# Routed experts with 1,632 slots, odd-sized ones as a double-width matmul, in a fused attention and mixture-of-experts kernel

## The chip, the cores and the metric

One core of one Trainium2 chip runs the whole program. The metric is the device time of one execution in microseconds (us). The kernel before takes 794.46 us, the median of 3 runs (794.2 to 794.81). A core has one matrix engine (TensorE, PE in the profile; its weight loads are listed apart as PEld), VectorE (DVE), ScalarE (ACT), GpSimd (POOL) and SyncE (SP), which here only issues transfers. Each engine works off its own list of instructions in order and waits on semaphores for the others.

## The reference

Three layers follow each other, all in fp32. The third is the one that the change touches: each of 1,536 tokens goes to the one of 8 experts whose logit is largest, and only that expert's two weight matrices (512 by 1024 and 1024 by 512) act on it.

```python
x = attention(q, k, v, lam)                 # (1536, 512), decayed, in blocks of 64
out1 = sum_e p[:, e] * (relu(x @ w1[e]) @ w2[e])          # 4 experts, every token
logits = out1 @ w_gate                      # (1536, 8)
expert = argmax(logits); gate = softmax(logits)[expert]
for e in range(8):
    xe = out1[expert == e]
    out[expert == e] = gate[expert == e] * (relu(xe @ w1b[e]) @ w2b[e])
```

With the reference's inputs the eight experts get 161, 102, 158, 127, 272, 269, 247 and 200 tokens.

## The kernel before

Every fp32 operand is split into a high part and a low part in a reduced format (names that end in h and l), and a product is three matmuls into one PSUM bank: high by high, low by high, high by low (`mm3`, L335). Attention and the first mixture fill the time up to about 604 us. Then the routed experts run one after the other, in what is called turns here, 0 to 7.

The tokens' rows are scattered into `bins` in memory, where each expert has a fixed number of slots. Turn 0 is always expert 0; the other seven are ranked by their number of tokens at run time, `BY_RANK` (L36) gives the slots by rank and `TURNS` (L37) the order. So the slots by turn, `CAPS`, are 256, 288, 128, 288, 256, 256, 256, 128: 1,856 in all. A token beyond its expert's slots goes to a loop at the end (L1042 onwards) that runs only where there are such tokens.

A turn has a first product (tiles `g`, or `gr` where the slots are 128) and a second. In the first, weights stand in the array and the slots' columns move past them: 8 banks of PSUM, each 12 matmuls as wide as the slots (`moe2_mm1`, L883). ACT takes relu out of each bank as the high part, DVE subtracts to get the low part (`relu_split`, L343). The second product has two forms. Where the slots fill whole tiles of 128 (`CAPS[e] <= 2 * P`, L1029), the slots stand and the weights move, 512 columns at a time (`moe2_mm2_rows`, tiles `zr`; 48 matmuls for 256 slots), and DVE applies the gate (L947). For 288 slots the weights stand again (`moe2_mm2`, tiles `z`, 4 banks), ACT copies each bank out, PE transposes it back (`yo`, L976) and DVE applies the gate (L978). The PSUM banks of both products come from one ring of three (`ps_mm`).

What else sets the order: between matmul groups the hooks (`hook1`, `hook2`, L999 and L1006) issue the weights' splits, each a copy on ACT (L161) and a subtraction on DVE (L163) of 512 columns, 16 for each expert. `hook1` runs after each of the 8 banks and asks for 2 splits of this turn's second weights; `hook2` runs four times in the second product and asks for the next turn's weights, after two calls also for half of the next turn's second weights where the form is `zr`. Raw weights wait in 6 buffers of 512 KB; a split that frees one makes SP issue the next load. `rows_T` (L870) transposes the next turn's rows on PE (`xt`), and ACT and DVE split them (`xgh`, `xgl`).

Of the kernel before, what the change touches and what calls it, by code (L numbers as in the profile page):

```python
# [18 lines left out]
P = 128  # L19
# [6 lines left out]
DM = H * D  # L26
KD = DM // P
E1, FF = 4, 1024
E2 = 8
HF = FF // 2  # L30
FC = HF // P
# [1 line left out]

BY_RANK = [288, 288, 256, 256, 256, 128, 128]  # L36
TURNS = [0, 5, 1, 2, 3, 4, 6]  # L37
CAPS = [256] + [BY_RANK[i] for i in TURNS]
NSS = [-(-c // P) for c in CAPS]
STS = [c // n for c, n in zip(CAPS, NSS)]  # L40
CAP, ST, NS = CAPS[0], STS[0], NSS[0]
MOST, NMOST = max(CAPS), max(NSS)
W = DM + 2
FAR = 1 << 20
OMAX = (N - min(CAPS[0], BY_RANK[0]) + P - 1) // P
# [4 lines left out]
def body(ctx: ExitStack, tc: tile.TileContext, lam, att, dp, w1a, w2a, wg, wgt, w1b, w2b, out):  # L50
    nc = tc.nc
    V, A, G, T, SP = nc.vector, nc.scalar, nc.gpsimd, nc.tensor, nc.sync
# [282 lines left out]
    def mm3(ps, parts, first, last):  # L335


        ops = [(l, rh) for (lh, ll), (rh, rl) in parts for l in (lh, ll)]
        ops += [(lh, rl) for (lh, ll), (rh, rl) in parts]
        for i, (l, r) in enumerate(ops):  # L340
            T.matmul(ps, l, r, start=first and i == 0, stop=last and i == len(ops) - 1)  # L341

    def relu_split(ps, tag, n, nm, pl, bufs, most=None):  # L343
        hh, hl = (
            pl.tile([P, most or n], F32R, tag=tag + x, name=nm + x, bufs=bufs)[:, :n]
            for x in "hl"
        )
# [289 lines left out]
    with tc.manual_schedule():  # L637
# [15 lines left out]
            out=upper, in_=upper, compare_op=ALU.is_ge, fill=1.0, base=0,  # L653
# [157 lines left out]
        y, z = NC - 2, NC - 1  # L811
# [19 lines left out]
        gx = z_ctx.enter_context(pool("gx", 2))  # L831

        def rows_tiles(e):
            return tuple(
                gx.tile([P, KD, MOST], F32R, tag="xg" + x, name=f"xg{x}{e}")[:, :, :CAPS[e]]
                for x in "hl"
            )

        def rows_split(hi, lo, ps):
            A.copy(out=hi, in_=ps)  # L840
# [2 lines left out]
        xg = {0: rows_tiles(0)}  # L843
# [4 lines left out]
        gp = z_ctx.enter_context(pool("gp", 2))  # L848
# [21 lines left out]
        def rows_T(e, s):  # L870
            if e >= E2:
                return
            if s == 0:
                xg[e] = rows_tiles(e)
            hi, lo = xg[e]
            st = STS[e]
            tr = ps_tr.tile([P, KD, P], F32, tag="tr", name=f"xt{e}_{s}")[:, :, :st]
            for d in range(KD):
                T.transpose(tr[:, d, :], xb_t[e][:st, s, d * P:d * P + P], ident[:st, :st])
            c = slice(s * st, s * st + st)  # L880
            rows_split(hi[:, :, c], lo[:, :, c], tr)

        def moe2_mm1(e, f):  # L883
            hi, lo = xg[e]
            k, c = 2 * (E1 + e) + f // FC, (f % FC) * P
            wh, wl = wt[0, k]
            n = CAPS[e]
            ps = ps_mm.tile([P, 512], F32, tag="mm", name=f"g{e}_{f}")
            mm3(
                ps[:, :n],  # L890
                [((wh[:, d, c:c + P], wl[:, d, c:c + P]), (hi[:, d, :], lo[:, d, :]))
                 for d in range(KD)],
                True, True,
            )
            return relu_split(ps[:, :n], "g", n, f"g{e}_{f}", gp, 2 * FC + 2, MOST)


        def moe2_mm1_rows(e, h, hook):
            hi, lo = xg[e]
            wh, wl = wt[0, 2 * (E1 + e) + h]  # L900
            n = CAPS[e]
            ps = ps_mm.tile([P, 512], F32, tag="mm", name=f"gr{e}_{h}")
            for d in range(KD):
                mm3(ps[:n], [((hi[:, d, :], lo[:, d, :]), (wh[:, d, :], wl[:, d, :]))],
                    d == 0, d == KD - 1)
                if d < KD - 1:
                    hook(h * KD + d)
            g = gp.tile([P, HF], F32, tag="gr", name=f"gr{e}_{h}")
            A.activation(out=g[:n], in_=ps[:n], func=AF.Relu)
            hook(h * KD + KD - 1)  # L910
            return g
# [13 lines left out]
        def moe2_mm2_rows(e, hs, y, hook):  # L925
            st, ns, xb = STS[e], NSS[e], xb_t[e]
            step = FC * ns // 2
            ps = [
                ps_mm.tile([P, 512], F32, tag="mm", name=f"zr{e}_{s}") for s in range(ns)
            ]  # L930
            i = 0
            for h in range(2):
                wh, wl = wt[1, 2 * (E1 + e) + h]
                for s in range(ns):
                    for f in range(FC):
                        hh, hl = hs[h * FC + f]
# [9 lines left out]
                    m = DM // 2 if e == E2 - 1 and s == ns - 1 else DM  # L946
                    V.tensor_scalar(  # L947
                        out=y[:st, s, :m], in0=ps[s][:st, :m], scalar1=gate, scalar2=None,
                        op0=ALU.mult,
                    )  # L950
                    if m < DM:
                        A.activation(
                            out=y[:st, s, m:], in_=ps[s][:st, m:], func=AF.Copy, scale=gate
                        )
                    scatter(out, xb.bitcast(I32)[:st, s, DM + 1:W], y[:st, s, :], N, "out")
            hook(3)


        def moe2_mm2(e, hs, m):
            n = CAPS[e]  # L960
            ps = ps_mm.tile([P, 512], F32, tag="mm", name=f"z{e}_{m}")
            c = slice(m * P, m * P + P)
            parts = []
            for f, (hh, hl) in enumerate(hs):
                wh, wl = wt[1, 2 * (E1 + e) + f // FC]
                parts.append(((wh[:, f % FC, c], wl[:, f % FC, c]), (hh, hl)))
            mm3(ps[:, :n], parts, True, True)
            yt = gp.tile([P, MOST], F32, tag="yt", name=f"yt{e}_{m}", bufs=3)
            A.copy(out=yt[:, :n], in_=ps[:, :n])
            return yt  # L970

        def moe2_out(e, yt, m, y):
# [9 lines left out]
            if m == KD - 1:  # L982
                for s in range(ns):
                    scatter(out, xb.bitcast(I32)[:st, s, DM + 1:W], y[:st, s, :], N, "out")

        load_rows(0)
        load_rows(1)
        raws[:] = [raw2] * 2 + [rawp] * 4
# [3 lines left out]
        for e in range(E2):  # L992
            k = 2 * (E1 + e)
            load_rows(e + 2)
            y = gp.tile([P, NMOST, DM], F32, tag="y", name=f"y{e}")
            hs = []
            turns = []

            def hook1(i):  # L999
                if late:  # L1000
                    late.pop()()
                split_to(1, k + 1, 2)
                if i == KD + 1 and turns:
                    hs.extend(turns.pop()())

            def hook2(i):  # L1006
                if turns:
                    hs.extend(turns.pop()())
                if late:
                    late.pop()()  # L1010
                if e == 0 and i == 0:
                    route_rest()
                if e + 1 < E2:
                    if i < NSS[e + 1]:
                        rows_T(e + 1, i)
                    if CAPS[e] <= 2 * P and i > 1:
                        split_to(1, k + 2, 3)
                    else:
                        split_to(0, k + 3, 2 if i == 0 else 3)

            if CAPS[e] <= P:
                for h in range(2):
                    g = moe2_mm1_rows(e, h, hook1)
                    turns.append(lambda h=h, g=g: moe2_turn(e, h, g))
            else:
                for f in range(2 * FC):
                    hs.append(moe2_mm1(e, f))
                    hook1(f)
            if CAPS[e] <= 2 * P:  # L1029
# [171 lines left out]
```

## Time and profile before

| | before |
|---|---|
| median of 3 runs | 794.46 us |
| profiled execution | 795.49 us |
| its span, first to last instruction | 793.7 us |
| PE busy in the span | 777.6 us (98%) |
| DVE busy in the span | 364.9 us (46%) |
| ACT busy in the span | 218.0 us (27%) |
| mean granted TensorE clock | 0.996 |

The span lies inside the profiled execution, 1.8 us shorter. PE's busy share is taken from records with modelled ends that overlap each other; the distance from the start of one matmul to the start of the next is what a matmul costs in a stream.

### The profile page before, as it was taken

To read this page: it belongs to the slowest core of one execution; us is meant where nothing else is said; L and a number is where in the kernel's file an instruction comes from. 1 tells how busy PE (TensorE), PEld (TensorE's weight loads), DVE (VectorE), ACT (ScalarE), POOL (GpSimd) and SP (SyncE) were. 2 spreads that over 40 slices of the span, in tenths; PEclk is the share of its full clock that TensorE was granted. 3 is DMA by queue.
4 is the path that set the end of the run, shared out by engine and by line. 5 is a ranking of instruction groups with operands and counts; after the bars stand their busy time and mean duration, and the time that the engine had idled before them with its cause. 6 is when DMAs were issued, how large, how long until landed. Compare 5 with 4: busy or idle time off the path is not lost. (4 is left out here: it accounts for less than half of the span.)

```text
span 793.7 us, 11237 instructions
## 1 busy us (share of the span) xinstructions
PE 777.6 (98%) x4458; PEld 649.4 (82%) x4458; DVE 364.9 (46%) x803; ACT 218.0 (27%) x440; POOL 112.1 (14%) x115
## 2 busy tenths in 40 slices
PE   7999999999999999999999999999999999999995
PEld 6788777887777777877777787878888898998884
DVE  5443212232332232233233233689877757677653
ACT  3222222111111221121022131011134546555552
POOL 4463201000110110010011020011120003121101
PEclk9999999999999999999999999999999999999998
DMA  8763273110100010011001012000023867766550
GB/s 271 262 211 122 69 255 130 40 54 1 53 28 27 27 53 27 0 54 54 0 27 54 26 40 67 0 27 27 29 82 132 290 207 264 247 214 225 182 189 24
DMA packets 25431, 81.20 MB, mean 102 GB/s; under 512 B 3164, under 2 KB 5212, under 8 KB 25248
## 3 DMA queue, kind: packets, MB, share of 16 engines
q1 hardware_dynamic: 23232, 74.15, 28.1%
q0 software_dynamic: 2144, 6.31, 2.0%
q8 instruction: 36, 0.59, 0.3%
q14 instruction: 19, 0.16, 0.1%
HBM read 69.40 MB, written 11.70 MB: 102 GB/s over the span
## 5 line engine op out<-in xcount | busy, mean ns | idle before, releaser
L341 PE MATMUL h<-xh,w0h 128*128 128x512 f32 (+1 forms) x432 | 158.3, 373 | 0.7 <-ACT xh L303 0.7
L341 PE MATMUL h<-xh,w0l 128*128 128x512 f32 (+1 forms) x432 | 157.1, 370 | 0.7 <-POOL w0l L163 0.7
L382 DVE SCALAR_TENSOR_TENSOR acc<-y,p_sb,acc 128x512 f32<-128x512 f32 x84 | 63.1, 751 | 124.4 <-PE y L341 122.3
L341 PE MATMUL h<-xl,w0h 128*128 128x512 f32 (+1 forms) x432 | 107.4, 370 | 0.0
L341 PEld LDWEIGHTS h<-xh,w0h 128*128 128x128 f32 x432 | 81.1, 188 | 17.0 <-ACT xh L303 0.9
L341 PEld LDWEIGHTS h<-xh,w0l 128*128 128x128 f32 x432 | 81.2, 188 | 16.4 <-POOL w0l L163 1.1
L341 PEld LDWEIGHTS h<-xl,w0h 128*128 128x128 f32 x432 | 76.2, 188 | 15.2
L348 ACT ACTIVATE ht_0h<-h 128x512 fp32r<-128x512 f32 (+1 forms) x27 | 14.9, 551 | 241.0 <-PE h L341 241.0
L163 POOL TENSOR_TENSOR w0l<-raw,w0h 128x512 fp32r<-128x512 f32 x17 | 22.7, 1340 | 252.1 <-ACT w0h L161 252.1
L161 ACT CAST w1h<-raw 128x512 fp32r<-128x512 f32 x96 | 54.3, 618 | 1.3 <-PE zr L341 1.3
L161 ACT CAST w0h<-raw 128x512 fp32r<-128x512 f32 x96 | 54.0, 620 | 0.5 <-DMA raw<-in_w1a 0.5
L163 DVE TENSOR_TENSOR w1l<-raw,w1h 128x512 fp32r<-128x512 f32 x80 | 52.5, 695 | 2.9 <-ACT w1h L161 2.9
L163 DVE TENSOR_TENSOR w0l<-raw,w0h 128x512 fp32r<-128x512 f32 x79 | 50.9, 687 | 5.8 <-ACT w0h L161 5.4
L341 PE MATMUL g<-xgh,w0h 128*128 128x256 f32 (+1 forms) x192 | 49.7, 289 | 0.6 <-DVE g_0l L349 0.3
L341 PE MATMUL g<-xgh,w0l 128*128 128x256 f32 (+1 forms) x192 | 49.3, 286 | 0.0
L96 POOL DMA_INDIRECT out<-y,xb x16 | 23.2, 1449 | 153.0 <-DVE y L947 64.8
L349 DVE SCALAR_TENSOR_TENSOR ht_0l<-h,ht_0h 128x512 fp32r<-128x512 f32 (+1 forms) x27 | 17.1, 632 | 59.1 <-ACT ht_0h L348 59.1
L341 PE MATMUL y<-w1h,ht_0h 128*128 128x512 f32 x96 | 39.4, 410 | 0.0
L341 PE MATMUL y<-w1h,ht_3l 128*128 128x512 f32 x96 | 39.2, 408 | 0.1
L434 DVE CUSTOM_DVE_ANT_0 jl<-acc,wgb 128x512 f32<-128x512 f32 x56 | 38.4, 685 | 0.8
L341 PE MATMUL y<-w1h,ht_2h 128*128 128x512 f32 x96 | 38.2, 398 | 0.0
L341 PE MATMUL y<-w1h,ht_2l 128*128 128x512 f32 x96 | 38.1, 397 | 0.0
(284 smaller groups left out, 1408.9 us busy)
## 6 DMA issues: line engine op xcount, KB each, us to landing
raw<-in_w1b SPq DMA_DIRECT2D x32, 512.0 KB, 5.4
raw<-in_w2b SPq DMA_DIRECT2D x32, 512.0 KB, 4.7
att<-in_att SPq DMA_DIRECT2D x24, 512.0 KB, 4.9
raw<-in_w2a SPq DMA_DIRECT2D x16, 512.0 KB, 3.6
raw<-in_w1a SPq DMA_DIRECT2D x14, 512.0 KB, 3.5
bins<-fill SPq DMA_DIRECT2D x1, 4626.0 KB, 21.8
xb<-bins SPq DMA_DIRECT2D x4, 514.0 KB, 5.4
wgb<-in_wgt SPq DMA_DIRECT2D x1, 2048.0 KB, 9.7
```

The lines of the kernel that those rows point to most:

```text
L96: i = G.indirect_dma_start(out=dst, out_offset=bass.IndirectOffsetOnAxis(ap=idx, axis=0), in_=src, in_offset=None, bounds_check=rows - 1, ...
L161: A.copy(out=hi, in_=t)
L163: (G if i < 3 else V if i >= 4 * ROUTED else los[i % 2]).tensor_tensor(out=lo, in0=t, in1=hi.bitcast(F32), op=ALU.subtract)
L341: T.matmul(ps, l, r, start=first and i == 0, stop=last and i == len(ops) - 1)
L348: A.activation(out=hh, in_=ps, func=AF.Relu)
L349: V.scalar_tensor_tensor(out=hl, in0=ps, scalar=0.0, in1=hh.bitcast(F32), op0=ALU.max, op1=ALU.subtract)
L382: V.scalar_tensor_tensor(out=acc[:, t, 0:DM], in0=ps, scalar=p_sb[:, t, e:e + 1], in1=acc[:, t, 0:DM], op0=ALU.mult, op1=ALU.add,)
L434: V.tensor_tensor_reduce(out=jl, in0=acc[:, t, 0:DM], in1=rt["wgb"][:, e, :], scale=1.0, scalar=0.0, op0=ALU.mult, op1=ALU.add, accum_out= ...
```

## The change

The slots become 176 for turn 0 and 288, 128, 288, 256, 208, 160, 128 for the others: 1,632. `WIDE` is true for more than 128 and less than 256 slots, turns 0, 5 and 6. For these the high and low activations lie side by side in one tile (`both`), so that `product` multiplies the high weights by both at once (one matmul of twice the slots) and the low weights by the high part (one matmul of the slots, into the first half of the bank): 2 matmuls for 3. The two halves of the bank must then be added: ACT copies the second half out, DVE adds the first (`s`), and relu and the low part read `s` from SBUF. They are put behind the copy and sum of the next bank, through the list `relu`. The wide turns' second product takes the transposed form (`z`). The other turns keep `mm3`. `zr` results are now scaled by the gate on ACT, not DVE. In wide turns `hook1` issues 1 split for each bank instead of 2, `hook2` 2 each time, and only turns with whole tiles (`BY_ROWS`) split the next turn's second weights ahead.

```diff
-BY_RANK = [288, 288, 256, 256, 256, 128, 128]
+BY_RANK = [288, 288, 256, 208, 160, 128, 128]
-CAPS = [256] + [BY_RANK[i] for i in TURNS]
+CAPS = [176] + [BY_RANK[i] for i in TURNS]
+BY_ROWS = [c % P == 0 for c in CAPS]
+WIDE = [P < c < 2 * P for c in CAPS]
...
+        def product(e, ps, parts):
+            n = CAPS[e]
+            if not WIDE[e]:
+                mm3(ps[:, :n], [(w, x[:2]) for w, x in parts], True, True)
+                return ps[:, :n]
+            for i, ((wh, wl), (hi, _, both)) in enumerate(parts):
+                T.matmul(ps[:, :2 * n], wh, both, start=i == 0, stop=False)
+                T.matmul(ps[:, :n], wl, hi, start=False, stop=i == len(parts) - 1)
+            s = gp.tile([P, MOST], F32, tag="yt", name=f"s{ps.name}", bufs=4)[:, :n]
+            A.copy(out=s, in_=ps[:, n:2 * n])
+            V.tensor_tensor(out=s, in0=ps[:, :n], in1=s, op=ALU.add)
+            return s
...
+            relu.append(finish)
+            while len(relu) > WIDE[e]:
+                relu.pop(0)()
...
-                    V.tensor_scalar(
-                        out=y[:st, s, :m], in0=ps[s][:st, :m], scalar1=gate, scalar2=None,
-                        op0=ALU.mult,
-                    )
+                    A.activation(out=y[:st, s, m:], in_=ps[s][:st, m:], func=AF.Copy, scale=gate)
...
-                split_to(1, k + 1, 2)
+                split_to(1, k + 1, 1 if WIDE[e] else 2)
...
-                    if CAPS[e] <= 2 * P and i > 1:
+                    if BY_ROWS[e] and i > 1:
                         split_to(1, k + 2, 3)
                     else:
-                        split_to(0, k + 3, 2 if i == 0 else 3)
+                        split_to(0, k + 3, 2 if i == 0 or WIDE[e] else 3)
```

In the listings that follow a row is the line, the instruction, output<-inputs and the output's size. The first place is PE at the start of turn 0's second product; before:

```order
L341 MATMUL zr_0_5123<-w1h_4976,g_0h 128x512
L341 MATMUL zr_0_5123<-w1h_4976,g_0l 128x512
L341 MATMUL zr_0_5123<-w1l_4977,g_0h 128x512
L341 MATMUL zr_0_5123<-w1h_4976,g_1h 128x512
L341 MATMUL zr_0_5123<-w1h_4976,g_1l 128x512
L341 MATMUL zr_0_5123<-w1l_4977,g_1h 128x512
```

The same place of the changed kernel, where `g_0` is the tile that holds both parts:

```order
L892 MATMUL z_0_5106<-g_0_4970,w1h_4971 128x352
L893 MATMUL z_0_5106<-g_0_4970,w1l_4972 128x176
L892 MATMUL z_0_5106<-g_1_4987,w1h_4971 128x352
L893 MATMUL z_0_5106<-g_1_4987,w1l_4972 128x176
L892 MATMUL z_0_5106<-g_2_5006,w1h_4971 128x352
L893 MATMUL z_0_5106<-g_2_5006,w1l_4972 128x176
```

Three matmuls of 512 columns have become two of 352 and 176, and one output bank now takes all 8 activation tiles in a row instead of 4.

The second place is DVE in turn 0's first product, from the last step of the routing's order (`nth`) on; before, `w1l` are splits of the second weights and `g_0l` the low part of bank 0:

```order
L601 TENSOR_SCALAR nth<-who 128x7
L349 SCALAR_TENSOR_TENSOR g_0l<-g_0_4959,g_0h 128x256
L163 TENSOR_TENSOR w1l_4977<-raw_4600,w1h_4976 128x512 x2
L349 SCALAR_TENSOR_TENSOR g_1l<-g_1_4984,g_1h 128x256
L163 TENSOR_TENSOR w1l_4977<-raw_4637,w1h_4976 128x512 x2
L349 SCALAR_TENSOR_TENSOR g_2l<-g_2_5007,g_2h 128x256
```

In the changed kernel `sg_0` is the sum of bank 0's halves:

```order
L605 TENSOR_SCALAR nth<-who 128x7
L896 TENSOR_TENSOR sg_0_4958_4967<-g_0_4958,sg_0_4958_4967 128x176
L167 TENSOR_TENSOR w1l_4972<-raw_4600,w1h_4971 128x512
L896 TENSOR_TENSOR sg_1_4975_4984<-g_1_4975,sg_1_4975_4984 128x176
L914 SCALAR_TENSOR_TENSOR g_0_4970<-sg_0_4958_4967,g_0_4970 128x176
L167 TENSOR_TENSOR w1l_4972<-raw_4600,w1h_4971 128x512
L896 TENSOR_TENSOR sg_2_4994_5003<-g_2_4994,sg_2_4994_5003 128x176
L914 SCALAR_TENSOR_TENSOR g_1_4987<-sg_1_4975_4984,g_1_4987 128x176
L167 TENSOR_TENSOR w1l_4972<-raw_4637,w1h_4971 128x512
```

Each bank now has two DVE instructions for one, a bank's low part stands behind the next bank's sum, and one split stands between banks for two, so the eighth split comes after the last bank instead of the fourth.

The third place is ACT between turns 4 and 5 in the changed kernel, where `w0h` and `w1h` are splits and `y<-zr` is the gate, which stood on DVE before:

```order
L165 CAST w0h_6349<-raw_6182 128x512 x2
L980 ACTIVATE y_6123<-zr_0_6294,xb_5604 128x512
L980 ACTIVATE y_6123<-zr_1_6295,xb_5604 128x512
L165 CAST w1h_6395<-raw_6206 128x512 x2
L165 CAST w1h_6395<-raw_6228 128x512
L895 COPY sg_0_6418_6427<-g_0_6418 128x208
```

The three splits and the copy of turn 5's bank 0 now queue behind the gate of the last `zr` bank.

## Rows read from the trace of the kernel before

**Rows 1.** The page: span, busy times, TensorE and its granted clock in 40 slices.

```profile
span 793.7 us, 11237 instructions
...
PE   7999999999999999999999999999999999999995
...
PEclk9999999999999999999999999999999999999998
```

**Rows 2.** Windows, turns 0, 2, 3, 5, 6, 7: length, engines' busy, clock, DMA share, GB/s.

```profile
610.47:634.09 23.62, 23.62 (x156) 21.37 (x157) 17.97 (x46) 13.64 (x31) 0.97 (x1) 1.00 0.75 259
...
660.96:675.26 14.30, 13.79 (x74) 11.07 (x72) 10.97 (x19) 11.21 (x23) 7.19 (x3) 1.00 0.91 300
675.26:703.20 27.94, 27.63 (x210) 27.31 (x209) 18.51 (x34) 14.65 (x31) 2.38 (x1) 1.00 0.61 215
...
726.93:750.22 23.29, 23.29 (x153) 21.10 (x152) 15.42 (x29) 12.55 (x26) 2.20 (x2) 1.00 0.61 214
750.22:773.08 22.86, 22.86 (x150) 20.71 (x148) 14.96 (x28) 12.51 (x27) 3.17 (x3) 1.00 0.58 201
773.08:793.70 20.62, 12.53 (x57) 9.46 (x55) 7.34 (x12) 5.00 (x9) 2.14 (x2) 0.86 0.07 28
```

**Rows 3.** Timeline of PE, turns 1 and 6: start, length, instruction, where stages begin.

```profile
634.09 0.29 PE L341 MATMUL g<-xgh,w0h 128*128 128x288 f32 x1
...
646.88 0.30 PE L341 MATMUL z<-g_0h,w1h 128*128 128x288 f32 x1
...
750.22 0.28 PE L341 MATMUL g<-xgh,w0h 128*128 128x256 f32 x1
...
761.53 0.40 PE L341 MATMUL zr<-w1h,g_0h 128*128 128x512 f32 x1
...
764.31 0.60 PE L879 MATMUL xt<-ident,xb 128*128 128x128 f32 x4
764.66 0.48 PE L341 MATMUL zr<-w1h,g_0h 128*128 128x512 f32 x1
```

**Rows 4.** Timeline of PE, narrow matmuls: the routing's logits, and transposes in turn 1.

```profile
577.79 0.95 PE L455 MATMUL lg<-wg_sb,xt 128*128 128x8 f32 x8
578.60 0.63 PE L442 MATMUL rtr<-ident,acc 128*128 128x128 f32 x4
...
653.68 0.49 PE L976 MATMUL yo<-ident,yt 128*96 128x128 f32 x3
653.93 0.38 PE L341 MATMUL z<-g_0h,w1h 128*128 128x288 f32 x1
```

**Rows 5.** Timeline of DVE, start of turn 0.

```profile
611.32 0.15 DVE L582 COPY count<-counts 128x8 f32<-128x8 f32 x1
...
613.01 0.42 DVE L349 SCALAR_TENSOR_TENSOR g_0l<-g,g_0h 128x256 fp32r<-128x256 f32 x1
613.35 1.28 DVE L163 TENSOR_TENSOR w1l<-raw,w1h 128x512 fp32r<-128x512 f32 x2
614.55 0.42 DVE L349 SCALAR_TENSOR_TENSOR g_1l<-g,g_1h 128x256 fp32r<-128x256 f32 x1
```

**Rows 6.** Timeline of ACT, turn 0, turn 2 and the last gate.

```profile
612.24 0.39 ACT L348 ACTIVATE g_0h<-g 128x256 fp32r<-128x256 f32 x1 [1.46 <-issue]
612.52 1.13 ACT L161 CAST w1h<-raw 128x512 fp32r<-128x512 f32 x2
...
661.26 3.22 ACT L161 CAST w1h<-raw 128x512 fp32r<-128x512 f32 x6
...
786.18 0.48 ACT L952 ACTIVATE y<-zr,xb 128x256 f32<-128x256 f32 x1 [4.18 <-DVE y L947]
```

**Rows 7.** Who waited for whom on PE and PEld, 610 to 790 us: total, times, longest.

```profile
PE g L341 <- DVE g_0l L349: 0.3, 1, 0.3
...
PEld zr L341 <- DVE gtl L841: 1.6, 3, 0.9
```

**Rows 8.** SP's own queue, who it waited for, 600 to 794 us.

```profile
SPq L135 <- DVE w0l L163: 88.5, 27, 11.0
```

More of the change, by code (lines that the diff above doesn't have):

```diff
@@ L341, in mm3, with relu_split @@
             T.matmul(ps, l, r, start=first and i == 0, stop=last and i == len(ops) - 1)
-    def relu_split(ps, tag, n, nm, pl, bufs, most=None):
+    def relu_split(ps, tag, n, nm, pl, bufs):
         hh, hl = (
-            pl.tile([P, most or n], F32R, tag=tag + x, name=nm + x, bufs=bufs)[:, :n]
+            pl.tile([P, n], F32R, tag=tag + x, name=nm + x, bufs=bufs)
             for x in "hl"
@@ L833, in rows_tiles @@
         def rows_tiles(e):
-            return tuple(
-                gx.tile([P, KD, MOST], F32R, tag="xg" + x, name=f"xg{x}{e}")[:, :, :CAPS[e]]
-                for x in "hl"
-            )
+            n = CAPS[e]
+            both = gx.tile([P, KD, 2 * MOST], F32R, tag="xg", name=f"xg{e}")[:, :, :2 * n]
+            return both[:, :, :n], both[:, :, n:], both
         def rows_split(hi, lo, ps):
@@ L874, in rows_T @@
                 xg[e] = rows_tiles(e)
-            hi, lo = xg[e]
+            hi, lo, _ = xg[e]
             st = STS[e]
@@ L881, in rows_T @@
             rows_split(hi[:, :, c], lo[:, :, c], tr)
+        def product(e, ps, parts):
+            n = CAPS[e]
+            if not WIDE[e]:
[8 more added lines that the diff above has]
+            return s
         def moe2_mm1(e, f):
-            hi, lo = xg[e]
+            hi, lo, both = xg[e]
             k, c = 2 * (E1 + e) + f // FC, (f % FC) * P
@@ L888, in moe2_mm1, with finish @@
             ps = ps_mm.tile([P, 512], F32, tag="mm", name=f"g{e}_{f}")
[L889 to L895, printed above, removed]
+            s = product(e, ps, [
+                ((wh[:, d, c:c + P], wl[:, d, c:c + P]),
+                 (hi[:, d, :], lo[:, d, :], both[:, d, :])) for d in range(KD)
+            ])
+            g = gp.tile([P, 2 * MOST], F32R, tag="g", name=f"g{e}_{f}", bufs=2 * FC + 2)
+            hh, hl = g[:, :n], g[:, n:2 * n]
+            def finish():
+                A.activation(out=hh, in_=s, func=AF.Relu)
+                V.scalar_tensor_tensor(
+                    out=hl, in0=s, scalar=0.0, in1=hh.bitcast(F32), op0=ALU.max,
+                    op1=ALU.subtract,
+                )
+            relu.append(finish)
+            while len(relu) > WIDE[e]:
+                relu.pop(0)()
+            return hh, hl, g[:, :2 * n]
         def moe2_mm1_rows(e, h, hook):
-            hi, lo = xg[e]
+            hi, lo, _ = xg[e]
             wh, wl = wt[0, 2 * (E1 + e) + h]
@@ L935, in moe2_mm2_rows @@
                     for f in range(FC):
-                        hh, hl = hs[h * FC + f]
+                        hh, hl = hs[h * FC + f][:2]
                         c = slice(s * st, s * st + st)
@@ L945, in moe2_mm2_rows @@
                     gate = xb[:st, s, DM:DM + 1]
-                    m = DM // 2 if e == E2 - 1 and s == ns - 1 else DM
-                    V.tensor_scalar(
-                        out=y[:st, s, :m], in0=ps[s][:st, :m], scalar1=gate, scalar2=None,
-                        op0=ALU.mult,
[L950 to L953, printed above, removed]
+                    m = DM // 2 if e == E2 - 1 and s == ns - 1 else 0
+                    if m:
+                        V.tensor_scalar(
+                            out=y[:st, s, :m], in0=ps[s][:st, :m], scalar1=gate, scalar2=None,
+                            op0=ALU.mult,
                         )
+                    A.activation(out=y[:st, s, m:], in_=ps[s][:st, m:], func=AF.Copy, scale=gate)
                     scatter(out, xb.bitcast(I32)[:st, s, DM + 1:W], y[:st, s, :], N, "out")
@@ L963, in moe2_mm2 @@
             parts = []
-            for f, (hh, hl) in enumerate(hs):
+            for f, h in enumerate(hs):
                 wh, wl = wt[1, 2 * (E1 + e) + f // FC]
[L966 to L969, printed above, removed]
+                parts.append(((wh[:, f % FC, c], wl[:, f % FC, c]), h))
+            s = product(e, ps, parts)
+            if WIDE[e]:
+                return s
+            yt = gp.tile([P, MOST], F32, tag="yt", name=f"yt{e}_{m}", bufs=4)
+            A.copy(out=yt[:, :n], in_=s)
             return yt
@@ L984, in moe2_out @@
                     scatter(out, xb.bitcast(I32)[:st, s, DM + 1:W], y[:st, s, :], N, "out")
+        relu = []
         load_rows(0)
@@ L1027, in body @@
                     hs.append(moe2_mm1(e, f))
+                    if f == 2 * FC - 1:
+                        while relu:
+                            relu.pop(0)()
                     hook1(f)
-            if CAPS[e] <= 2 * P:
+            if BY_ROWS[e]:
                 moe2_mm2_rows(e, hs, y, hook2)
```

## The prediction

> **What bounds the kernel now.** I read the page first: PE is busy in every slice from the second to the last but one, at the upper clock level throughout [rows 1]. So the change is worth what it takes off PE, less what other engines then fail to hide. Next the windows, one for each turn of the routed stage [rows 2]: in the turns that change (0, 5, 6) PE is busy for the whole 23.62, 23.29 and 22.86 us, DVE for 18.0, 15.4 and 15.0, ACT for at most 13.6. PE is the bound, but DVE in turn 0 is only 5.6 us behind, and the change takes work from PE and gives some to DVE. What waits there are on PE and its weight loads from 610 us on are short and name DVE, the largest 1.6 us in all [rows 7]. PE, DVE and ACT wait for no transfer there: it is SP that waits for DVE to free a raw buffer, 88.5 us behind first-weight splits alone [rows 8], and turn 2 took in 300 GB/s [rows 2] without a wait for data.
>
> **What a matmul costs.** From start to start. 256 columns: turn 6's first product is 96 matmuls in 761.53 - 750.22 = 11.31 us, 0.118 each. 288 columns: turn 1's, 96 in 646.88 - 634.09 = 12.79, 0.133 each. 512 columns: 12 in 764.31 - 761.53 = 2.78, 0.232 each [rows 3]. On the line between the last two, 320, 352 and 416 columns are 0.147, 0.161 and 0.190. The narrow partners (160, 176, 208) are not in the trace. Below: by columns alone, 0.46 ns each as at 256, they are 0.074, 0.081, 0.096. Above: the 0.118 of 256 columns. In between stands the row for the logits: 8 matmuls of only 8 columns take 578.60 - 577.79 = 0.81 us, 0.101 each [rows 4], so there is a floor that is not the columns'; each brings a new 128-column weight load, as each narrow partner does. I take 0.101 for all three.
>
> The Trainium skill, TensorE: Matmul & The Clock Gate, section LDWEIGHTS, gives a load the number of its columns over 1.2 ns, whatever the rows; for 128 columns an estimate from that page is 0.107 us. It speaks against a part of this change, since narrower slots then save nothing on the second matmul; the logits' row agrees within 6%. By it the sum below would lose 192 times 0.006, 1.2 us more.
>
> **Part by part: PE.** A wide turn has 32 pairs in each product, 64 in all. Turn 0: 64 x (0.161 + 0.101) = 16.8 us. Turn 5: 64 x 0.291 = 18.6. Turn 6: 64 x 0.248 = 15.9. Before, each was 96 x 0.118 + 48 x 0.232 = 22.4. New are 8 transposes back for each turn; three cost 653.93 - 653.68 = 0.25 us [rows 4], so 0.67. Saved: 22.4 - 16.8 - 0.7 = 4.9, then 3.1 and 5.8, together 13.9 us.
>
> Smaller items. Selecting and placing turn 0's rows is narrower (176 for 256): the last selection, one pair of placing matmuls, one cast and one subtraction stand in a chain before turn 0 and each loses some 0.05 to 0.08 us; 0.3. Row transposes for turns 5 and 6 have 104 and 80 columns for 128, which cost 0.35 for four [rows 3]: 0.1 and 0.25, 0.35 together. The gate leaves DVE in turn 2, so turn 3's bank 0 is split earlier, and the one wait of PE on `g_0l`, 0.3 us [rows 7], goes (in turn 3 PE is 0.3 short of fully busy [rows 2]). Gain in all: 13.9 + 0.3 + 0.35 + 0.3, about 14.9 us.
>
> **Part by part: what DVE and ACT then fail to hide.** In a stream a 512-column split is 0.60 on DVE (two in 614.55 - 613.35) and a 256-column one 0.34 (613.35 - 613.01) [rows 5], so 176 columns are 0.26, 160 0.24, 208 0.29. On ACT it is 0.52 for 512 (six in 3.22) and 0.28 for 256 (612.52 - 612.24) [rows 6], so 0.20 for 176. One bank of turn 0's first product is then 4 x 0.262 = 1.05 on PE, 0.60 + 2 x 0.26 = 1.12 on DVE, 0.92 on ACT. In turn 5: 1.16, 1.18, 0.98. In turn 6: 0.99, 1.08, 0.88. DVE is the slower one, by little, and the ring of three banks lets PE run three banks ahead. What counts is the end of the stage: the second product's first bank reads all 8 tiles and, for its last pair, the eighth split, which now stands last on DVE.
>
> Turn 0: DVE comes late, since the routing's order keeps it until 613.01 [rows 5], 612.4 after the narrower casts; 8 x 0.60 + 16 x 0.26 = 9.0 us more make 621.4. PE starts at 610.2 and could finish this bank at 610.2 + 8.4 + 2.1 = 620.7. It ends about 621.9: 1.2 us lost. Turn 6: DVE starts some 1.5 us in (a bank, ACT's copy), has 9.0 us with one gate of turn 5, so 10.5; PE could be through at 10.1 and ends near 10.9: 0.8 lost. Turn 5: turn 4 still splits three ahead, so five splits are left, and DVE is done with them by bank 4; the end of the chain (copy, sum, relu, low part: some 1.6 us) lies behind six pairs of PE, 1.7 us. The gate on ACT waits for turn 4's last bank, and behind it queue three splits and bank 0's copy; the sum comes some 3.3 us into the turn, when PE needs that bank again at 3.5. Lost: 0. Turn 7: turn 6 no longer splits ahead, so its first ACT relu and DVE's `gtl` queue behind all 8 second-weight splits. Turn 2 is in that place already and takes 14.3 us; without its three row transposes (0.35 x 96/128 each, 0.8) and one more transpose back (0.25) that is 13.2, against the 12.5 for which PE is busy in turn 7 [rows 2]. With DVE later than there I take 1.2 lost.
>
> In the second products DVE has per bank a sum (0.26), a gate (0.34), two splits (1.2) and in some a row split (0.47 for 384 columns, on the same line), 1.8 to 2.3 us, against PE's 2.0 to 2.7 with transposes: hidden. In turn 0 eight small steps of the routing's rest come on top, as long as the eight of its order, 1.7 us [rows 5]; DVE is then about a bank behind, which the ring takes; if it didn't, turn 0 would cost up to 1 us more. Turn 1 loses its splits from turn 0 but has 1.6 us of PE for 1.57 of DVE in each of four banks: hidden. Loads: 8 pieces of 512 KB in some 17 us are 240 GB/s, under turn 2's 300: hidden. Losses: 1.2 + 0.8 + 1.2 = 3.2 us; the bounds are none, if the waits overlap better, and twice that.
>
> **The sum.** 14.9 - 3.2 = 11.7 us. The span goes from 793.7 to 782.0 and the profiled execution from 795.5 to 783.8. The runs' median lies 1.0 below the profiled one, so 782.7.
>
> **Rivals.**
>
> 1. The narrow partners cost their columns alone. 64 x (0.027 + 0.020 + 0.005) = 3.3 us less PE; half of it lies in first products where DVE decides, so 1.7, and with half of the losses gone 779.4. For it: nothing shows that this operand format loads as slowly as that of the logits; the PEld records overlap too much to say. Against: the floor in rows 4.
> 2. DVE becomes the bound of the wide turns. If sums, subtractions and splits don't stream but cost their full length (0.42 at 256 columns and 1.28 - 0.60 = 0.68 at 512 in rows 5, so 0.34 for 176), a bank of turn 0 is 1.36 on DVE for my 1.12, 0.24 more, and so in the others: over 8 banks 1.9 us in turn 0, 1.9 in turn 6 and over 5 banks 1.2 in turn 5, together 5.0: 787.7. For it: each sum now waits for ACT's copy and each relu for the sum. Against: rows 5 show them streaming, and the delay by one bank keeps the two from meeting.
> 3. The clock falls: slower than before. The stalls come at the second product's start in turns 0 and 6 and in turn 7. If they are long enough for the granted clock to go to 1.2 GHz for half of the 51 us of matmuls in the wide turns (16.8 + 18.6 + 15.9), that half takes twice as long, 25 us more: 808. It decides against the change when about 12 us run at the lower level. For it: the last window, where PE stops for 8 us, has clock 0.86. Against: 1.00 in turns 2 and 3, with 0.5 and 0.3 us of PE idle [rows 2], and my stalls are about 1 us. The Trainium skill, TensorE: Matmul & The Clock Gate, section HAM oscillation, has kernels whose engine fell back to half rate between bursts of matmuls.
> 4. The slots don't suffice, and the change doesn't do what it says: one expert with a token too many runs the loop at the end, with its fill, 12 scatters and 4 MB of weights, none of it hidden. At turn 2's 300 GB/s the weights alone are 14 us, and 12 scatters at 0.97 (turn 0's one in rows 2) are 12: at least 808. Against: the counts fit (161 in 176, 200 in 208, 158 in 160; 127 in 128 as before).
>
> **Chances.** Forecast 0.63, rival 1 0.12, rival 2 0.20, rival 3 0.03, rival 4 0.02. What can be told from no change is 0.2%, 1.6 us. The first three are all faster, less 0.02 for a sum of losses that I don't see, hence faster 0.93, same 0.02, slower 0.05. The forecast's own bounds: the narrow partner at 0.118 costs 64 x 3 x 0.017 = 3.2 us more, no losses 3.2 us less. The range reaches to rival 1 with some over and just past rival 2: 778.5 to 788.
>
> **What would show it.** Matmul starts in the wide turns: the narrow partner takes 0.10 us (right), under 0.09 (rival 1) or 0.12 (my upper bound). Turns 0, 5 and 6 take about 19.5, 19.8 and 17.7 us; turn 7 is 1.2 longer. PE waits for DVE at the first `z` bank of turns 0 and 6, on the last `w1l` or `g`, and hardly in turn 5 or inside later banks; waits at each bank would be rival 2. The clock stays at 1.00 in turns 0 to 6. I would be wrong if PE waited for a raw load anywhere from turn 1 on, or if the wide matmul were off the line of the other widths.

## The result, and the profile after

| | before | after |
|---|---|---|
| median of 4 runs each | 794.53 us (794.2 to 794.81) | 785.67 us (785.13 to 787.97) |
| ratio, 95% interval | 1 | 0.9895 (0.9883 to 0.9907) |
| profiled execution / its span | 795.49 / 793.7 us | 785.84 / 783.9 us |
| PE busy | 777.6 us | 766.7 us |
| DVE / ACT busy | 364.9 / 218.0 us | 368.8 / 226.8 us |

The change makes the kernel 8.9 us faster, by 1.05%. I had forecast 782.7 us: sign and mechanism hold, the gain is smaller. All ratios here leave out executions that ran far longer than the rest of the same kernel: six of the twelve of `slots_only` (815 to 817 us, mean granted clock 0.966 to 0.968) and two of the four of `partner64` (798 and 799 us, 0.978 and 0.975), of which no trace is on record, so that where their clock fell stays open, one of `kept` (4055.82 us) and two of the kernel before (1657.25 and 2689.3 us).

The page of the profile after, against [rows 1]: span, busy times, PE and its granted clock in 40 slices.

```profile
span 783.9 us, 11270 instructions
...
PE 766.7 (98%) x4434; PEld 643.6 (82%) x4434; DVE 368.8 (47%) x842; ACT 226.8 (29%) x479; POOL 118.0 (15%) x115
...
PE   7999999999999999999999999999999999999995
...
PEclk9999999999999999999999999999999999999999
```

PE is still busy in all slices but the first and the last, so the span has again shrunk by nearly what PE saves (9.8 us for 10.9 us less of busy time). The windows of the turns, to compare with [rows 2]: start and end, length, busy time of PE, PEld, DVE, ACT and POOL (with instructions), granted clock, DMA share, GB/s. They are turns 0, 3, 5, 6 and 7.

```profile
609.41:629.49 20.08, 19.64 (x147) 19.19 (x147) 18.43 (x56) 14.29 (x37) 1.19 (x2) 1.00 0.79 273
...
670.92:698.21 27.29, 27.29 (x210) 27.27 (x209) 17.87 (x33) 15.22 (x33) 3.27 (x1) 1.00 0.67 219
...
722.07:742.60 20.53, 20.53 (x143) 20.29 (x142) 15.99 (x37) 14.46 (x36) 1.19 (x2) 1.00 0.68 240
742.60:761.68 19.08, 18.33 (x143) 17.71 (x141) 16.80 (x41) 14.38 (x37) 3.02 (x2) 1.00 0.73 226
761.68:783.90 22.22, 13.07 (x61) 9.55 (x58) 8.78 (x17) 8.12 (x16) 7.26 (x3) 0.93 0.11 40
```

Turn 0 loses 3.54 us, turn 5 2.76 and turn 6 3.78, turn 3 0.65. Turn 7 grows by 1.6. Turns 1, 2 and 4 are within 0.3 us of before. In turns 0 and 6 PE is no longer busy throughout, and DVE stands within 1.7 and 2.3 us of the turn's length. Turn 0 also starts 1.06 us earlier, 0.66 of it already at the row transpose (`rtr`) at 600 us, where PE has run no edited instruction yet; in the profiles of the kernels below this start lies anywhere from 608.7 to 610.1. From that `rtr` to turn 0 it is 9.79 us before and 9.39 after, and 9.38 to 9.40 in six of the profiles below that have 176 slots; so 0.40 us belong to the change.

The timeline of PE in the kernel after (start, length, line, output<-inputs, size): a stretch of turn 0's first product, the end of the first output bank of turn 6's second product, and turn 7's.

```profile
612.22 0.35 PE L892 MATMUL g<-xg,w0h 128*128 128x352 f32 x1
612.41 0.24 PE L893 MATMUL g<-xg,w0l 128*128 128x176 f32 x1
612.49 0.35 PE L892 MATMUL g<-xg,w0h 128*128 128x352 f32 x1
...
752.51 0.24 PE L893 MATMUL z<-g,w1l 128*128 128x160 f32 x1
753.04 0.42 PE L892 MATMUL z<-g,w1h 128*128 128x320 f32 x1 [0.29 <-DVE g L914]
...
753.68 0.41 PE L892 MATMUL z<-g,w1h 128*128 128x320 f32 x1 [0.15 <-ACT w1h L165]
754.41 0.34 PE L893 MATMUL z<-g,w1l 128*128 128x160 f32 x1 [0.31 <-DVE w1l L167]
...
769.72 0.50 PE L345 MATMUL zr<-w1h,gtl 128*128 128x512 f32 x1 [0.70 <-DVE gtl L844]
```

A pair starts every 0.27 us in turn 0: over the first product the ordinary spacing is 0.2733, for my 0.262. In turn 5 it is 0.300 (for 0.291), in turn 6 0.259 (for 0.248). Taking off 0.161, 0.190 and 0.147 for the wide matmul leaves 0.112, 0.110 and 0.112 for the narrow one, the same for 176, 208 and 160 columns; the wide one's share is still taken from the prediction's line, no row gives it by itself. (Between two starts the record shows 0.19 after a wide one and 0.08 after a narrow one, so only the sum of the two says what a pair costs.) The rows of turn 6 show the wait at the end of the stage: the first output bank took 3.56 us, from 751.03 to 754.59, and the second 2.11, and the waits name the last `g`, the last `w1h` and the last `w1l`.

Whom PE waited for in the routed stage of the kernel after, against [rows 7]: engine, what waits, for what, total us, times, longest.

```profile
PE zr L345 <- DVE gtl L844: 1.2, 2, 0.7
PE rank L500 <- DVE oh L472: 0.6, 1, 0.6
PE z L893 <- DVE w1l L167: 0.6, 2, 0.3
...
PE z L892 <- DVE g L914: 0.3, 1, 0.3
PE z L892 <- ACT w1h L165: 0.2, 1, 0.2
```

On PE there are no waits for a sum (`sg`), for a bank or for a transfer; its weight loads (PEld) wait once for a `sg`, 0.2 us, and once for the second product's sum (`sz`), 0.3. DVE in the kernel after, turn 0, against [rows 5]:

```profile
612.56 0.33 DVE L896 TENSOR_TENSOR sg<-g,sg 128x176 f32<-128x176 f32 x1
612.81 0.33 DVE L914 SCALAR_TENSOR_TENSOR g<-sg,g 128x176 fp32r<-128x176 f32 x1
613.06 0.69 DVE L167 TENSOR_TENSOR w1l<-raw,w1h 128x512 fp32r<-128x512 f32 x1
613.66 0.34 DVE L896 TENSOR_TENSOR sg<-g,sg 128x176 f32<-128x176 f32 x1
...
764.18 4.89 DVE L167 TENSOR_TENSOR w1l<-raw,w1h 128x512 fp32r<-128x512 f32 x8
768.99 0.68 DVE L844 TENSOR_TENSOR gtl<-gt,gth 128x512 fp32r<-128x512 f32 x1
```

From one bank's sum to the next it is 613.66 - 612.56 = 1.10 us, without an idle step: the three instructions stream, each starting before the one ahead has run its full length. The last two rows are turn 7's queue: eight splits ahead of `gtl`.

### The profile page after: what moved, and what is told of

It reads as the page before. It is cut to its first block, busy times and chain, and to the rows that moved or that the text cites. A ratio compares the mean times of both kernels' runs of the same rounds, so it can differ in the third digit from the quotient of the medians.

```text
span 783.9 us, 11270 instructions
## 1 busy us (share of the span) xinstructions
PE 766.7 (98%) x4434; PEld 643.6 (82%) x4434; DVE 368.8 (47%) x842; ACT 226.8 (29%) x479; POOL 118.0 (15%) x115
## 4 chain that ended last, share of the span: by engine, by line
PE 74%; issue 17%; DVE 4%; POOL 2%; DMA 2%; ACT 1%; SPq 0%; POOLq 0%; DVEq 0%; ACTq 0%
PE y L345 34%; PE h L345 34%; POOL out L100 2%; PE xo L299 1%; PE qk L240 1%; PE xo L293 1%; DMA raw<-in_w1a 1%; DMA att<-in_att 1%; DVE w1l L167 1%; PE u L321 1%; DVE w0l L167 1%; PE lg L459 0%; DVE sg L896 0%; PE rtr L446 0%; DVE xg L844 0%
## 5 line engine op out<-in xcount | busy, mean ns | idle before, releaser
L100 POOL DMA_INDIRECT out<-y,xb x16 | 29.2, 1824 | 138.0 <-DVE y L1006 84.9
L345 PE MATMUL y<-w1l,ht_3h 128*128 128x512 f32 x96 | 38.0, 396 | 0.1
L345 PE MATMUL g<-xg,w0h 128*128 128x288 f32 (+1 forms) x192 | 38.1, 293 | 0.0
```

The costliest lines, as they stand in the source:

```text
L100: i = G.indirect_dma_start(out=dst, out_offset=bass.IndirectOffsetOnAxis(ap=idx, axis=0), in_=src, in_offset=None, bounds_check=rows - 1, ...
```

## The experiments

Each kernel is the changed one with the edit shown. Its ratio is to the kernel before, on the same chip.

**Narrower slots alone** (`slots_only`): 1,632 slots, but three matmuls for each product as before. The edit also puts relu back to the same bank and two splits to each hook; the second products of turns 0, 5 and 6 keep the transposed form.

```diff
-WIDE = [P < c < 2 * P for c in CAPS]
+WIDE = [False for c in CAPS]
```

> The slots of the change, but no activations side by side: the odd-sized turns keep three matmuls (160, 176 or 208 columns each) and relu at once. Theory A (below some 0.113 us a matmul costs its weight load, not its columns): 192 matmuls x 0.113 and 0.7 of transposes are what 256 slots cost before, so turns 0, 5 and 6 stay at 22.5 to 23.5 us; small gains of 1.3 us (head, row transposes, turn 3) against 1.6 us of new wait in turn 7: 794.8 us, 793 to 797. Theory B (columns alone, 0.46 ns each): turns 0, 5 and 6 lose 6, 3 and 7.5 us, about 778.

Measured: ratio 0.9987 (0.9976 to 0.9997). The first products of turns 0, 5 and 6 take 10.80, 10.74 and 10.95 us for 96 matmuls, 0.112 to 0.114 each, whether the slots are 176, 208 or 160. Its PE timeline in turn 0:

```profile
609.90 0.28 PE L345 MATMUL g<-xg,w0l 128*128 128x176 f32 x1
610.01 0.28 PE L345 MATMUL g<-xg,w0h 128*128 128x176 f32 x1
610.12 0.27 PE L345 MATMUL g<-xg,w0l 128*128 128x176 f32 x1
```

Against 0.118 at 256 columns that is 3 to 5% less for 19 to 38% fewer columns. Slots by themselves are worth almost nothing: turns 0, 5 and 6 take 23.09, 22.65 and 22.59 us, 0.3 to 0.6 less than before.

**Side by side alone** (`wide_only`): the old 256 slots in turns 0, 5 and 6, and pairs of 512 and 256 columns.

```diff
-BY_RANK = [288, 288, 256, 208, 160, 128, 128]
+BY_RANK = [288, 288, 256, 256, 256, 128, 128]
...
-CAPS = [176] + [BY_RANK[i] for i in TURNS]
+CAPS = [256] + [BY_RANK[i] for i in TURNS]
...
-BY_ROWS = [c % P == 0 for c in CAPS]
+BY_ROWS = [i not in (0, 5, 6) and c % P == 0 for i, c in enumerate(CAPS)]
-WIDE = [P < c < 2 * P for c in CAPS]
+WIDE = [i in (0, 5, 6) for i, c in enumerate(CAPS)]
```

> The old 256 slots in turns 0, 5 and 6, with activations side by side (matmuls of 512 and 256 columns) and the transposed second product. Theory A (a pair is worth only what it saves in weight loads that columns don't cover; at 256 nothing): 0.232 + 0.118 = 0.350 a pair against 3 x 0.118 = 0.354; plus 0.7 us of transposes for each of three turns and 1.6 us of wait in turn 7, less 0.6 in turn 3: 797 us, 795.5 to 799. Theory B (two matmuls for three pay by themselves): under 791.

Measured: ratio 1.0058 (1.0045 to 1.0071), slower, median 798.85 us. PE in its turn 5:

```profile
726.67 0.39 PE L892 MATMUL g<-xg,w0h 128*128 128x512 f32 x1
726.90 0.28 PE L893 MATMUL g<-xg,w0l 128*128 128x256 f32 x1
727.02 0.40 PE L892 MATMUL g<-xg,w0h 128*128 128x512 f32 x1
```

A pair takes 0.35, as much as three matmuls at 0.118. So side by side saves nothing at 256 columns, and the waits and the transposes back are left over. The gain of the change belongs to the two parts together. A wide matmul's price still goes with its columns (0.133 us at 288, 0.232 at 512), a narrow one's no longer does (0.112 to 0.114 at 160 to 208), so there only the number of matmuls counts: narrow slots bring down the columns of the wide matmul, and the pair takes one matmul in three away.

**Is the partner's price its columns?** (`partner64`): the narrow matmul cut to 64 columns.

```diff
-                T.matmul(ps[:, :n], wl, hi, start=False, stop=i == len(parts) - 1)
+                T.matmul(ps[:, :64], wl, hi[:, :64], start=False, stop=i == len(parts) - 1)
```

> The change, with the second matmul of each pair (low weights by high activations) cut to 64 columns, which leaves out part of that product. Theory A (the partner costs its weight load): pairs in the second products stay at 0.272, 0.30 and 0.26 us (turns 0, 5, 6) and the time at 785.7, within 1. Theory B (it costs its columns): a pair loses 0.04 to 0.07 us, 64 pairs in each of three turns, about half of it hidden by DVE: 779 to 781.

Measured: 784.85 and 785.43 us; turns 0, 5 and 6 take 19.95, 20.38 and 19.04 for 20.08, 20.53 and 19.08. PE in its turn 0:

```profile
610.86 0.19 PE L893 MATMUL g<-xg,w0l 128*128 128x64 f32 x1
...
611.13 0.19 PE L893 MATMUL g<-xg,w0l 128*128 128x64 f32 x1
```

A pair still takes 0.27, and a whole turn saves 0.04 to 0.15 us where theory B wanted 1.3 to 2.2. So with two thirds of the columns gone next to nothing is saved: the partner's price isn't its columns. That it is its weight load is my reading and not shown: no run changes the load by itself, and another fixed cost of a matmul in this format would give the same rows. Nor does every load of 128 columns cost that much: four transposes of the tokens' rows, each with such a load of its own, take 764.66 - 764.31 = 0.35 us [rows 3], 0.09 each.

**Relu not put behind** (`relu_now`).

```diff
-            while len(relu) > WIDE[e]:
+            while relu:
```

> The change, but relu and the low part right behind the same bank's sum. Theory A (the delay is what keeps DVE from waiting for ACT): DVE waits about 0.35 us in each bank for ACT's relu, 1.47 us a bank against PE's 1.05 to 1.1 in turns 0 and 6, 1.5 against 1.2 in turn 5 while it still splits: turns 0 and 6 some 2.8 us longer each, turn 5 some 1 us: 791 to 792 us. Theory B (the ring of three banks hides it): 785.7, within 0.8.

Measured: ratio 1.0148 (1.0133 to 1.0163), 805.92 us: slower than before, and more than three times the loss that I expected. DVE in its turn 0:

```profile
613.34 0.33 DVE L896 TENSOR_TENSOR sg<-g,sg 128x176 f32<-128x176 f32 x1
614.09 0.34 DVE L914 SCALAR_TENSOR_TENSOR g<-sg,g 128x176 fp32r<-128x176 f32 x1 [0.42 <-ACT g L913]
614.60 0.69 DVE L167 TENSOR_TENSOR w1l<-raw,w1h 128x512 fp32r<-128x512 f32 x1 [0.17 <-ACT w1h L165]
615.21 0.33 DVE L896 TENSOR_TENSOR sg<-g,sg 128x176 f32<-128x176 f32 x1
```

A bank takes DVE 1.87 us for 1.10. DVE waits 0.42 for ACT's relu, and a second time, 0.17, for the weight's copy that stands on ACT behind that relu. The other 0.18 is overlap of one instruction with the next, which is gone where a wait stands between them. Turns 0, 5 and 6 are 7.2, 4.6 and 7.9 us longer. What PE waited for, two rows of its list:

```profile
PE g L892 <- DVE sg L896: 5.3, 10, 0.6
PE z L892 <- ACT w1h L165: 3.1, 4, 0.8
```

PE now waits at ten of the 24 sums of the first products, and at none in the changed kernel, and stands still for longer. Behind such gaps its clock went down (windows of the same kernel in turns 0 and 6; clock is the third number from the end):

```profile
612.00:626.00 14.00, 9.96 (x61) 8.31 (x59) 9.53 (x23) 8.14 (x23) 0.00 (x0) 1.00 0.81 266
626.00:630.00 4.00, 3.70 (x17) 3.46 (x18) 2.91 (x12) 1.82 (x4) 0.00 (x0) 0.59 0.50 164
...
770.00:775.00 5.00, 4.28 (x17) 3.93 (x18) 2.98 (x6) 2.49 (x6) 0.00 (x0) 0.51 0.42 139
```

That is mostly the lower level, 1.2 GHz, for 4 us after a stretch in which PE was busy for 9.96 of 14, and again in turn 6 (0.51 here, 0.81 in the 5 us behind). What these windows lack of full clock, 4 x 0.41 + 5 x 0.49 + 5 x 0.19, is 5.0 us: by this estimate up to a quarter of the 20 us of loss is the clock and the rest the waits. My third rival can happen; in the changed kernel's first profile, with its shorter waits, the clock stays at 1.00 in these turns.

**The gate back on DVE** (`gate_dve`).

```diff
-                    if m:
-                        V.tensor_scalar(
-                            out=y[:st, s, :m], in0=ps[s][:st, :m], scalar1=gate, scalar2=None,
-                            op0=ALU.mult,
+                    m = m or DM
+                    V.tensor_scalar(
+                        out=y[:st, s, :m], in0=ps[s][:st, :m], scalar1=gate, scalar2=None,
+                        op0=ALU.mult,
+                    )
+                    if m < DM:
+                        A.activation(
+                            out=y[:st, s, m:], in_=ps[s][:st, m:], func=AF.Copy, scale=gate
                         )
-                    A.activation(out=y[:st, s, m:], in_=ps[s][:st, m:], func=AF.Copy, scale=gate)
```

> The change, with the gate of the row-form turns back on DVE. Theory A (moving it freed DVE ahead of turn 3's first banks): turn 3 is back at 27.9 us from 27.3, turn 5 perhaps 0.3 longer: 786.3 us. Theory B (it buys nothing): 785.7.

Measured: ratio 0.9921 (0.9909 to 0.9933), for 0.9895 and 0.9906 (0.989 to 0.9921) of the changed kernel on two other chips: too near to tell from the whole time, all the more as four of its six executions fall into the longer of the two groups of times that the section on the clock describes. By turns it can be told: turn 3 goes from 27.29 back to 27.94 us, and turn 5 from 20.53 to 20.37. The gate's move is worth 0.65 us in turn 3 and costs 0.16 in turn 5, where I had expected turn 5 to be longer without it.

**Two mends of the waits.** `halves_first` begins two output banks of a wide turn's second product with the first four activation tiles, and finishes them one after the other, so that the last tile and the last split are needed later.

```diff
...
+        def moe2_begin(e, hs):
+            begun = []
+            for m in range(2):
...
+                pairs(e, ps, parts[:FC], True, False)
+                begun.append((ps, parts[FC:]))
+            return begun
...
-                    yt = moe2_mm2(e, hs, m)
+                    yt = moe2_end(e, *begun[m]) if m < len(begun) else moe2_mm2(e, hs, m)
```

> The change, with the second product of the wide turns begun on two banks: first four pairs of bank 0, first four of bank 1, then the rest of bank 0, of bank 1. Theory A (the wait in turns 0 and 6 is only for the last tiles and the eighth split, which come 1 to 1.5 us late): turn 0 0.9 us shorter, turn 6 1.2: 783.6 us. Theory B (DVE's throughput bounds these turns, so the wait comes back in the next banks): 785.7.

`one_split` issues one split, not two, at each of turn 2's and turn 7's hooks, so that `gtl` doesn't queue behind eight.

```diff
-                split_to(1, k + 1, 1 if WIDE[e] else 2)
+                split_to(1, k + 1, 1 if WIDE[e] or CAPS[e] <= P else 2)
```

> The change, with one split per hook instead of two in the first product of the turns of 128 slots (2 and 7). Theory A (turn 7's first relu and gtl only queue behind eight splits issued early): turn 7 1.4 us shorter, turn 2 0.5: 783.8 us. Theory B (DVE is behind anyway and the splits are needed as soon): 785.7, the wait moves to the second-weight splits.

`both_mends` has both edits.

> Both of the last two edits together. If each removes its own wait: 781.7 us, and PE waits nowhere in turns 0 to 7 for more than 0.3 us. If DVE is the bound: over 785.

Measured: 0.989 (0.987 to 0.9911), 0.9883 (0.9866 to 0.9899) and 0.9869 (0.9849 to 0.9888). The intervals reach over that of the change; the turns tell more. With `halves_first` turn 0 takes 19.67 us (0.4 less) and turn 6 18.08 (1.0 less); with `one_split` turn 7 takes 21.19 (1.0 less) and turn 2 14.07 (0.2 less). So the waits of these places are real, and 2.6 us of them can be had back, about two thirds of what I expected of the two edits (4.0). With both edits PE waits nowhere in turns 0 to 7 for more than 0.3 us, as expected. The profile of `both_mends` showed something else: turn 0 took 21.6 us, with the clock at 0.50 for its first 4 us.

**The clock before turn 0** (`after_again`, the changed kernel once more, and `kept`, with 8 and 12 more empty matmuls where PE waits for the routing).

```diff
-        keep_up(4)
+        keep_up(12)
...
-        route_choose(z, lambda: (first_T(1), first_sel(y)))
+        route_choose(z, lambda: (first_T(1), keep_up(12), first_sel(y)))
```

> The change once more, unaltered, as the measure for the next three. Some executions lie near 785.5 us with a mean granted clock of 0.998 and some near 788 with 0.992: 785.1 to 788.5 here too.

> The change with 8 more empty matmuls in PE's gap before the last transposes of the routing and 12 in the gap before its last rank, both while PE waits for DVE. Theory A (the executions near 788 us are those in which the clock fell to 1.2 GHz after these gaps, at the end of the routing and in turn 0): no execution over 786.5, mean clock 0.996 or more in all. Theory B (the fall has another cause): the same two groups as without the edit.

Measured: 0.9906 (0.989 to 0.9921) and 0.9892 (0.9875 to 0.991). The changed kernel has two groups of times, and here the profile fell into the longer one. Its windows:

```profile
605.00:606.00 1.00, 0.37 (x5) 0.20 (x5) 0.89 (x5) 0.00 (x0) 0.00 (x0) 1.00 0.00 0
...
607.00:608.00 1.00, 1.00 (x8) 0.97 (x8) 0.82 (x7) 0.00 (x0) 0.15 (x1) 0.50 0.00 0
609.00:612.00 3.00, 3.00 (x15) 2.97 (x15) 2.39 (x10) 1.12 (x4) 0.97 (x1) 0.50 0.46 175
612.00:615.00 3.00, 3.00 (x19) 3.00 (x18) 2.06 (x7) 1.85 (x5) 0.00 (x0) 0.78 0.37 97
```

Two matmuls of the same stretch, which place turn 0's rows, show what one costs at the lower level:

```profile
607.05 0.41 PE L573 MATMUL px<-sel,al 128*128 128x176 f32 x1
607.26 0.41 PE L573 MATMUL px<-sel,ah 128*128 128x176 f32 x1
```

The windows of `kept`:

```profile
605.00:606.00 1.00, 1.00 (x18) 1.00 (x18) 0.72 (x5) 0.00 (x0) 0.00 (x0) 1.00 0.00 0
...
609.00:612.00 3.00, 3.00 (x23) 3.00 (x23) 2.76 (x13) 1.59 (x5) 0.97 (x1) 1.00 0.46 175
```

In `after_again` PE stands still for 0.63 us before the last ranks, and soon after the clock is at 0.50, the lower level, until the middle of turn 0's first product: that takes 10.35 us for 8.82. A matmul of 176 columns starts 0.21 us after the one ahead there, for 0.11 at 1.00. `kept` fills the gap, and its clock stays at 1.00. Of the changed kernel's ten executions four took 787.7 to 789.0, and of the 23 of the four kernels before this section (`gate_dve` to `both_mends`) twelve are in such a longer group, with a mean clock of 0.990 to 0.994; of the eleven of the kernels with the filling (`kept` and the two below) none is, each lies within 1.4 us of the lowest of its kernel. What isn't settled: the same gap stands in the changed kernel's first profile, whose clock stays at 1.00, and one of 0.5 us in the kernel before, which shows no such group in its runs here. So the filling keeps the clock up, but which executions fall without it is open.

**All of it, and GpSimd** (`both_kept` is `both_mends` with the empty matmuls; `pool_eighth` gives in addition two of the eight subtractions in turns 0 and 6 to GpSimd, and one in turn 5).

```diff
-    def split_to(w, k, most=1):
+    def split_to(w, k, most=1, on_pool=False):
...
-            (G if i < 3 else V if i >= 4 * ROUTED else los[i % 2]).tensor_tensor(
+            (G if i < 3 or on_pool else V if i >= 4 * ROUTED else los[i % 2]).tensor_tensor(
...
-                split_to(1, k + 1, 1 if WIDE[e] else 2)
+                split_to(1, k + 1, 1 if WIDE[e] or CAPS[e] <= P else 2, WIDE[e] and i in (3, 6))
```

> These empty matmuls together with the second product begun on two banks and one split per hook in turns 2 and 7. Theory A: all executions near 782.7 us, none over 784. Theory B: two groups, near 782.7 and 786.

> As the kernel before it, and in the first products of the wide turns the subtractions of the splits asked for after banks 3 and 6 go to GpSimd. Theory A (DVE is what turns 0 and 6 still wait for): 0.4 us shorter in each, 782 us. Theory B (GpSimd's slower subtraction, 1.34 us against 0.69, or its queue of scatters comes late): 783 to 786.

Measured: `both_kept` 0.9856 (0.9842 to 0.9871), 782.96 us: below the changed kernel's 0.9906 (0.989 to 0.9921) and `kept`'s 0.9892 (0.9875 to 0.991) on that chip, and the best of all. Against `kept` it is 2.6 us, what the two mends save in the turns. `pool_eighth` 0.9871 (0.9857 to 0.9886): no gain, each of its four executions is longer than each of `both_kept`'s. In its turn 6, GpSimd and then DVE:

```profile
748.89 1.32 POOL L167 TENSOR_TENSOR w1l<-raw,w1h 128x512 fp32r<-128x512 f32 x1
```

```profile
748.14 0.31 DVE L922 SCALAR_TENSOR_TENSOR g<-sg,g 128x160 fp32r<-128x160 f32 x1
...
748.63 1.77 DVE L922 SCALAR_TENSOR_TENSOR g<-sg,g 128x160 fp32r<-128x160 f32 x1
```

A DVE instruction that takes 0.31 us elsewhere takes 1.77 while GpSimd subtracts, and ends 0.2 us after it. So DVE isn't relieved of 0.6 us, it is held for 1.46. Not every instruction is held. In turn 0 the same kernel has:

```profile
618.94 1.47 POOL L167 TENSOR_TENSOR w1l<-raw,w1h 128x512 fp32r<-128x512 f32 x1 [2.08 <-ACT w1h L165]
```

```profile
619.18 0.32 DVE L904 TENSOR_TENSOR sg<-g,sg 128x176 f32<-128x176 f32 x1
619.43 1.43 DVE L922 SCALAR_TENSOR_TENSOR g<-sg,g 128x176 fp32r<-128x176 f32 x2
```

The sum (`sg`), one of whose two inputs is a PSUM bank, takes its usual 0.32 beside GpSimd; the low part, with both inputs in SBUF, is held until GpSimd is done. The Trainium skill, GPSIMD Engine Reference, section Specifications, says that GpSimd's way to SBUF is shared with VectorE and that they contend where DVE has two SBUF inputs; the DVE instruction that is held has two, and the trace agrees. Turn 6 takes 18.67 us for 18.06.

## Why the prediction was right, and where it was off

- **The pair and the slots.** Two matmuls for three, at narrower slots, take 2.8 to 3.8 us off each of the three turns, and PE bounds the kernel before and after. Right.
- **The narrow partner at 0.101.** Mis-sized, and the larger part of what is missing: the pairs leave 0.110 to 0.112 for it, so 64 x (0.011 + 0.009 + 0.011) = 2.0 us. I took it from the logits' row, which has another operand format; the upper bound, 0.118, was nearer. The step itself, that the price isn't the columns', is shown by `slots_only` and `partner64`; that it is the weight load's is argued, not shown, and the floor differs by format (0.09 for the transposes of [rows 3], 0.101 for the logits, 0.110 to 0.114 here). The Trainium skill, TensorE: Matmul & The Clock Gate, section LDWEIGHTS, would have put it at an estimated 0.107; the 0.110 to 0.112 agree within 5%, nearer than my row.
- **Losses of 3.2 us.** They came to about 4.0, at the places that were named. Turn 0 0.9 for 1.2 (its first output bank took 3.14 us, the second 2.23); turn 6 1.5 for 0.8 (3.56 against 2.11); turn 7 1.6 for 1.2; turn 5 none. In turn 6 DVE begins its sums 2.25 us into the turn, not 1.5: behind turn 5's last sum and gate and two splits that I had left out. `halves_first` and `one_split` show these waits by taking 1.4 and 1.0 us of them away.
- **Smaller items.** Turn 3 gained 0.65 for 0.3, and `gate_dve` shows that the gate's move is all of it. The start of turn 0 is 1.06 earlier for 0.3; only 0.40 of it belongs to the change, the rest lies ahead of PE's first edited instruction and is luck of this profile.
- **The sum.** The span shrank by 9.8 us where 11.7 were forecast. The 1.9 us between are 2.0 (partner) + 0.8 (losses) - 0.8 (start) - 0.35 (turn 3) = 1.65, and 0.25 of rest. The median misses by more, 785.67 for 782.7: I had also taken off the 1.0 us by which the profiled execution lay above the median before, and after it lies only 0.2 above. That step had no other ground than one execution.
- **The signs.** The clock at 1.00 in turns 0 to 6 (in this profile), the waits at the first `z` bank on the last `w1l` and `g`, and no wait for a raw load came as said. Turns 0, 5 and 6 took 20.1, 20.5 and 19.1 us for 19.5, 19.8 and 17.7. Whether the wide matmul is on the line of the other widths no run shows by itself.
- **Rival 1**, the columns alone, is refuted: 64 columns cost within 3 ns a pair of what 160 to 208 cost. **Rival 2**, no streaming, is refuted by DVE's 1.10 us for a bank, where it wanted 1.36, and by the absence of waits at the sums. **Rival 4** is refuted: no loop at the end is in the trace.
- **Rival 3**, the clock, is half true, in a place that I hadn't named: not at the new waits, but in the routing before turn 0, in four of the changed kernel's ten executions, at 3 us and not 25. `relu_now` shows that waits within the wide turns can bring it too once they are longer.

## What to carry to other kernels

Before narrowing a matmul, look at what one costs from start to start at the narrow width: where the price no longer falls with the columns, fewer columns give nothing, and only fewer matmuls do, which is why one edit that gains 0.1% alone and one that loses 0.6% alone gain 1.05% together. Where two engines hand work to and fro for each bank, put the second step behind the next bank's first one and look at what else queues on both: here the order alone was worth some 20 us, up to 5 of them by the clock. Price the last operand of the stage, since the next stage's first bank asks for all of them at once.

## What the runs showed of the hardware

- A matmul with a new 128-column load takes 0.112 to 0.114 us from start to start at 160 to 208 columns in this format (`slots_only`), 0.118 at 256. Cut from 176 to 64 columns, the second of a pair leaves the pair at 0.27 us (`partner64`). At the lower clock level 176 columns take 0.21 (`after_again`).
- A two-input subtraction on GpSimd (1.32 us) holds a DVE instruction with both inputs in SBUF until it ends: 1.77 us for 0.31. One with an input in PSUM isn't held: 0.32 (`pool_eighth`).
- The clock can fall to 0.50 behind a gap on PE of only 0.6 us where PE's work before it is small matmuls with other short gaps; it came in some executions and not in others of the same kernel, and none in eleven with the gaps filled.
